# A PSUM bank for each half of the array's rows: dense products of a pre-LN block from paired turns to one list woven through attention scores

## The chip, the cores and the metric

The kernel runs on one core of a Trainium2 chip. The metric is the device time of one execution in microseconds, the median of the runs shown. The profiled execution is one further run of the same program, taken by the hardware profiler.

## What is computed

One transformer block in float32, for 2048 tokens of width 512: layer norm, attention with 32 query heads of width 16 that share one key and one value head, output projection and residual; then layer norm, a gated GELU feed-forward of width 1792 and residual.

```python
q = (x @ wq).reshape(B, S, H, Dh)           # x: layer norm of A_x; S 2048, D 512, H 32, Dh 16
k, v = x @ wk, x @ wv                       # one head for all 32
p = softmax(einsum("bhqd,bkd->bhqk", q, k) * Dh ** -0.5)
h = A_x + einsum("bhqk,bkd->bhqd", p, v).reshape(B, S, 512) @ wo
z = layernorm(h)
h2 = h + (gelu(z @ w_gate) * (z @ w_up)) @ w_down        # F 1792
```

## The kernel before

The 2048 query rows are handled in four **blocks** of 512. In a block, attention goes through 8 groups of 4 heads and, in a group, through 16 slices of 128 keys. A **score** (`scores`, two matmuls at L329, on rows 0 to 49 and 64 to 113 of the array at once, followed by one exponential of 128 x 1024 on ScalarE, L333) does two heads of one slice, so 32 scores make a group and 256 a block; the whole kernel has 1024. Scores go through two PSUM buffers of two banks each. `weigh` (L337) multiplies a finished pair of scores with the values, as 8 short matmuls into the one bank `acc`; at the end of a group `evacuate` copies `acc` (L350), sends it through DRAM to turn it (SP's DMAs at L351 and L361), and the sums are inverted, multiplied and split into a high and a low float32r part on VectorE (L366 to L383).

The **dense** part (`dense`) of a block is output projection, layer norm, transposes of the normalised rows (`x_turn`, L565), 14 slices of the feed-forward (`up`, a gate and an up product each), and the down products in runs of 4, 4, 4 and 2 slices. Products take each operand as high and low part, three terms for each chunk of 128 of the contraction. Weights are parted on GpSimd during block 0's attention, stored to DRAM (`w1_d`, `w2_d`) and loaded again for each block by SP (`load_w1`, `load_w2`, lines L470 and L475).

PE, ScalarE, GpSimd, and here SP and VectorE too, execute in the order in which the program issues. The dense part of block b is woven into the scores of block b + 1; that of the last block stands alone in the tail (`solo`, full array, L512; projection at L622). In the weave a matmul uses half of the array's 128 rows, and two run side by side. `duo` (L490) does two products at once: in the first turn rows 0 to 63 serve the first product's bank and rows 64 to 127 the second's, in the second turn it is the other way round, so that no bank is written by both halves at once. Between the turns VectorE reads one element of the second bank (`mark`, L498), which orders the turns; the turns lie in different **chunks**. A turn has 12 **steps** of two matmuls (6 for the last run of down products).

The order of the work around the change is written out in `run`: a group of 32 scores has six chunks of 6, 5, 5, 6, 5, 5 scores (`SIZES`), and `LONG`, `LAST` and `SHORT` say how many dense steps follow each score of a chunk. At the end of a chunk all finished pairs are weighed (`finish`), in the last chunk of a group all there are. The kinds of chunk of a block are a list: 4 long for the projection, one "gap" with transposes, the long ones of the feed-forward, 2 short. A block's dense part starts at chunk 3 of the next block for block 0 and at chunk 2 for the others (`LEAD`). `gates` (tanh on ScalarE, L690, and the products behind it, L691, L692, L112, L113) are opened at the end of the chunk after. Three PSUM banks (tag "d", `psum1`) serve the dense products; with four for scores and one for `acc` that makes eight.

The program runs on after the check of a bound (`bound_flag`); the second path, with exact maxima, isn't taken with these inputs.

Of the kernel before, what the change touches and what calls it, by code (L numbers as in the profile page):

```python
# [26 lines left out]
PB = 5  # L27
# [11 lines left out]
BOUND_STEPS = ((0, 10), (0, 14))  # L39

CUT, EDGE, GAP, HOLD = -1, -2, -3, -4
# [3 lines left out]
def kernel(  # L45
# [59 lines left out]
    w1_d = dram.tile([FC, P, 2, 2, DC, P], F32R, name="w1_d")  # L105
# [37 lines left out]
    def run(outer, first):  # L143
# [10 lines left out]
        def psum1(name):  # L154
            return ps.tile([P, T], F32, tag="d", bufs=width, name=name)
# [164 lines left out]
        o_blk, pair, outs, last_out = {}, [None], [], []  # L320
# [27 lines left out]
        def evacuate(b, g, acc):  # L348
            oT = sb.tile([P, T], F32, tag="oT", bufs=2, name=f"oT_{b}_{g}")
# [29 lines left out]
            def piece(t):  # L379
                sl = slice(t * P, (t + 1) * P)  # L380
                hi, lo = o_blk[b]
                invert(t)
                nc.vector.tensor_tensor(  # L383
                    oc[:, 0, sl], oc[:, 0, sl], oc[:, 1, sl], op=ALU.mult
                )
                split(nc.vector, hi[:, c, sl], lo[:, c, sl], oc[:, 0, sl])

# [4 lines left out]
            if b == NB - 1 and g == NG - 1:  # L392
                last_out.append(piece)
            elif k == 1:

                outs.extend([[] for _ in range(4 if b == 0 else 1)])
                outs.extend([partial(invert, t), partial(invert, t + 1)] for t in (0, 2))
                outs.append([divide])
            if b == 0 and g == NG - 1:
                while outs:  # L400
                    take_out()

# [3 lines left out]
        def part_weights(pw):  # L406
# [25 lines left out]
            def store_1(f, k, both):  # L432
                nc.gpsimd.dma_start(
                    w1_d[f, :, :, k].bitcast(F32),
# [33 lines left out]
        def load_w1(b, f):  # L468
            w = db.tile([P, 2, 2, DC, P], F32R, tag="w1", bufs=2, name=f"w1_{b}_{f}")
            nc.sync.dma_start(w.bitcast(F32), w1_d[f].bitcast(F32))  # L470
            return w[:, 0], w[:, 1]

        def load_w2(b, j):
# [4 lines left out]
            return w[:, :, 0], w[:, :, 1]  # L478

        def duo(names, terms):  # L480

            banks = [psum1(n) for n in names]
            n = len(terms[0])
            for turn in range(2):
                for i in range(n):
                    for a in range(2):
                        k = (turn + a) % 2
                        lhsT, rhs = terms[k][i]
                        rows = slice(64 * a, 64 * a + 64)
                        nc.tensor.matmul(  # L490
                            banks[k], lhsT[rows], rhs[rows], start=(turn == 0 and i == 0),
                            stop=(turn == 1 and i == n - 1), skip_group_check=True,
                        )
                    yield 1
                if turn == 0:

                    mark = sb.tile([P, 1], F32, tag="mark", bufs=2, name=f"mark_{names[1]}")
                    nc.vector.tensor_copy(mark, banks[1][:, :1])  # L498
                    yield CUT
            return banks  # L500

        tail_ps = None

        def tail_bank(name):
            return tail_ps.tile([P, T], F32, tag="t", bufs=5, name=name)

        def solo(names, terms):
            banks = []
            for name, ts in zip(names, terms):
                bank = tail_bank(name)  # L510
                for i, (lhsT, rhs) in enumerate(ts):
                    nc.tensor.matmul(bank, lhsT, rhs, start=(i == 0), stop=(i == len(ts) - 1))  # L512
# [4 lines left out]
        def dense(b, tail=False):  # L517

            o_hi, o_lo = o_blk[b]
            product = solo if tail else duo  # L520
            xbs = {}

            def load_x(t):
                xbs[t] = db.tile([P, D], F32, tag="xb", bufs=2, name=f"xb_{b}_{t}")
                nc.sync.dma_start(xbs[t], x_t[:, b * TB + t, :])

            if not tail:
                load_x(0)
                load_x(1)
            xT_hi = db.tile([P, DC, T], F32R, tag="x2h", bufs=1, name=f"x2h_{b}")  # L530
            xT_lo = db.tile([P, DC, T], F32R, tag="x2l", bufs=1, name=f"x2l_{b}")
            w1 = {0: load_w1(b, 0), 1: load_w1(b, 1)}
            if b == 0:
                yield 0
            w2 = {}
            hs, xns, held = {}, {}, {}

            def project(t0):
                terms = []
                for t in (t0, t0 + 1):  # L540
                    sl = slice(t * P, (t + 1) * P)
                    terms.append([
                        (ot[:, c, sl], wt[:, c, :])
                        for c in range(DC)
                        for ot, wt in ((o_hi, wo_hi), (o_hi, wo_lo), (o_lo, wo_hi))
                    ])
                banks = yield from product([f"pp_{b}_{t0}", f"pp_{b}_{t0 + 1}"], terms)
                held[t0], held[t0 + 1] = banks

            def residual(t0):  # L550
                for t in (t0, t0 + 1):
                    hs[t] = db.tile([P, D], F32, tag="h", bufs=4, name=f"h_{b}_{t}")
                    nc.vector.tensor_tensor(hs[t], held.pop(t), xbs.pop(t), op=ALU.add)
                scaled = []
                for t in (t0, t0 + 1):
                    xns[t] = db.tile([P, D], F32, tag="xn2", bufs=2, name=f"xn2_{b}_{t}")
                    scaled.append(layer_norm(db, xns[t], hs[t], f"2_{b}_{t}"))
                return scaled

            def x_turn(t):  # L560

                bank = tail_bank if tail else psum1
                pt = bank(f"pxt_{b}_{t}").rearrange("p (c q) -> p c q", c=DC)
# [4 lines left out]
                if tail:  # L568
                    first_part = partial(nc.scalar.activation, hi, pt, AF.Copy)
                else:  # L570
                    first_part = partial(nc.vector.tensor_copy, hi, pt)
                return first_part, partial(
# [3 lines left out]
            def start():  # L576
                yield from project(0)
                for step in residual(0):
                    step()
                load_x(2)  # L580
                load_x(3)
                yield CUT
                second = project(2)
                for n in second:
                    if n == CUT:
                        yield EDGE
                        for part in x_turn(0):
                            part()
                    yield n
                parts = x_turn(1)  # L590

                behind.extend([*residual(2), *parts])
                yield GAP
                two = [x_turn(t) for t in (2, 3)]
                for i in range(2):
                    for parts in two:
                        parts[i]()
                yield CUT

            def start_tail():  # L600

                xp, xn, h = (
                    sb.tile([P, TB, D], F32, tag="p", bufs=PB, name=f"{n}p_{b}")
                    for n in ("x", "xn", "h")
                )
                for t in range(TB):
                    nc.sync.dma_start(xp[:, t, :], x_t[:, b * TB + t, :])

                pps = [psum1(f"pp_{b}_0")]
                pps.extend(tail_bank(f"pp_{b}_{t}") for t in range(1, TB))  # L610

                def add_x(t):
                    nc.tensor.matmul(pps[t], ident, xp[:, t, :], start=False, stop=False)

                def project_part(t, cs, start):
                    terms = [
                        (ot[:, c, t * P : (t + 1) * P], wt[:, c, :])
                        for c in cs
                        for ot, wt in ((o_hi, wo_hi), (o_hi, wo_lo), (o_lo, wo_hi))
                    ]  # L620
                    for i, (lhsT, rhs) in enumerate(terms):
                        nc.tensor.matmul(  # L622
                            pps[t], lhsT, rhs, start=start and i == 0,
                            stop=not start and i == len(terms) - 1,
                        )

                def norm(t):
                    scaled[t] = layer_norm(db, xns[t], pps[t], f"2_{b}_{t}", on_act=True)

                piece, scaled = last_out.pop(), {}  # L630
                for t in range(TB):
                    hs[t], xns[t] = h[:, t, :], xn[:, t, :]
                    project_part(t, range(DC - 1), True)
                for t in range(TB):
                    piece(t)
                    add_x(t)
                    project_part(t, (DC - 1,), False)
                    if t == 2:
                        norm(0)
                for t in range(1, TB):  # L640
                    norm(t)
# [624 lines left out]
```

## Time and profile before

| | us |
|---|---|
| median of 3 runs | 1448.79 (1447.65 to 1449.84) |
| the profiled execution | 1448.96 |
| its span, first to last instruction | 1446.9 |
| PE busy in it | 1406.3 |
| ScalarE busy | 1038.8 |
| VectorE busy | 533.4 |

Mean granted TensorE clock in it: 0.999. Times in the profile are microseconds from the span's start unless marked ns. PE is TensorE's matmuls, PEld its weight loads, DVE VectorE, ACT ScalarE, POOL GpSimd, SP the engine that issues most DMAs. A group of instructions is a line with engine, operation, output<-inputs and count; then busy time and mean ns of one; then idle time of the engine just before them and what ended it. In a chain or a timeline the first two columns are start and duration. A matmul's duration (0.39 us) is longer than the distance to the next one, as they are pipelined.

### The profile page before, as it was taken

Reading aid. Unit: us, or ns where it says so; the run is one execution under the profiler, and the core shown is the slowest. Engines: PE = TensorE matmul, PEld = TensorE weight load, DVE = VectorE, ACT = ScalarE, POOL = GpSimd, SP = SyncE. Lnnn points to the kernel's source line nnn. Section 1 sums busy time; section 2 is a strip of 40 time slices with the busy share of each in tenths; the row PEclk is TensorE's granted clock in tenths of the full one; section 3 lists DMA queues with packets and bytes.
Section 4 is the critical chain, followed back from the end, with each engine's and each line's share of the span. In section 5 each row is a group of like instructions: output and inputs, shape, how many; then the busy total and the mean of one; then the engine's idle time right before and its main releaser. Section 6 shows DMA issues by size and latency. Waiting matters only on the chain.

```text
span 1446.9 us, 24766 instructions
## 1 busy us (share of the span) xinstructions
PE 1406.3 (97%) x10420; PEld 749.3 (52%) x10420; DVE 533.4 (37%) x925; ACT 1038.8 (72%) x1147; POOL 223.1 (15%) x305
## 2 busy tenths in 40 slices
PE   6999999999999999999999999999999999999998
PEld 5433333334555555554555555554555555556886
DVE  7403131223342424333242424323251422426665
ACT  6699999996777877777777777777777777772000
POOL 5588868601000000000000000000000000001000
PEclk9999999999999999999999999999999999999999
DMA  4467667631422333122333232212323323233552
GB/s 155 140 210 238 230 211 233 207 124 56 148 82 93 107 114 113 57 74 95 124 107 109 90 114 87 83 52 100 136 86 113 113 85 108 106 134 104 188 188 76
DMA packets 58863, 180.54 MB, mean 125 GB/s; under 512 B 8540, under 2 KB 8540, under 8 KB 51544
## 3 DMA queue, kind: packets, MB, share of 16 engines
q1 hardware_dynamic: 48912, 144.79, 29.6%
q0 software_dynamic: 9760, 34.08, 7.1%
q8 instruction: 84, 1.38, 0.4%
q14 instruction: 35, 0.29, 0.1%
q10 hardware_dynamic: 72, 0.00, 0.0%
HBM read 131.13 MB, written 47.71 MB: 124 GB/s over the span
## 4 chain that ended last, share of the span: by engine, by line
PE 76%; ACT 16%; issue 3%; DVE 2%; DMA 1%; POOL 0%; SPq 0%; ACTq 0%; POOLq 0%; DVEq 0%
PE acc L337 31%; PE s L329 17%; ACT p L333 15%; PE pu L490 5%; PE pd L490 5%; PE pg L490 4%; PE pq L182 3%; PE pd L512 3%; PE pg L512 2%; PE pu L512 2%; PE pp L490 1%; PE pk L1053 1%; DMA acc_d<-oT 1%; DVE oc L366 0%; DMA w<-w_d 0%
## 5 line engine op out<-in xcount | busy, mean ns | idle before, releaser
L333 ACT ACTIVATE p<-s 128x1024 f32<-128x1024 f32 x1024 | 967.8, 1036 | 257.6 <-PE s L329 257.1
L337 PE MATMUL acc<-p,v_sb 128*32 128x512 f32 x4096 | 493.9, 598 | 0.0
L329 PE MATMUL s<-qg,kaug 50*128 50x512 f32 x1984 | 391.5, 435 | 15.0 <-ACT p L333 11.1
L329 PEld LDWEIGHTS s<-qg,kaug 50*128 50x128 f32 x1984 | 169.8, 184 | 304.3 <-ACT p L333 173.2
L337 PEld LDWEIGHTS acc<-p,v_sb 128*32 128x32 f32 x4096 | 110.2, 109 | 240.4 <-issue 230.7
L490 PE MATMUL pu<-x2h,w 64*128 64x512 f32 x672 | 231.6, 391 | 0.0
L490 PE MATMUL pg<-x2h,w 64*128 64x512 f32 x672 | 231.5, 391 | 0.0
L122 POOL TENSOR_SCALAR rstd<-mv 128x1 f32<-128x1 f32 x16 | 3.5, 220 | 998.0 <-DVE mv L120 997.8
L490 PE MATMUL pg<-x2l,w 64*128 64x512 f32 x336 | 131.3, 391 | 0.0
L490 PE MATMUL pu<-x2l,w 64*128 64x512 f32 x336 | 131.3, 391 | 0.0
L490 PEld LDWEIGHTS pu<-x2h,w 64*128 64x128 f32 x672 | 124.9, 186 | 11.6
L490 PEld LDWEIGHTS pg<-x2h,w 64*128 64x128 f32 x672 | 124.8, 186 | 10.6
L490 PE MATMUL pd<-w,gh 64*128 64x512 f32 x672 | 105.4, 391 | 0.0
L690 ACT ACTIVATE ga<-ga 128x512 f32<-128x512 f32 x56 | 36.3, 647 | 89.6 <-DVE ga L685 89.6
L682 DVE COPY g<-pg 128x512 f32<-128x512 f32 x56 | 38.5, 688 | 128.5 <-PE pg L490 121.1
L490 PEld LDWEIGHTS pd<-w,gh 64*128 64x128 f32 x672 | 63.3, 185 | 14.6 <-issue 0.7
L366 DVE RECIPROCAL oc<-oc 128x128 f32<-128x128 f32 x64 | 56.0, 919 | 37.4 <-DMA oc<-acc_d 36.3
L498 DVE COPY mark_pu<-pu 128x1 f32<-128x1 f32 x42 | 6.6, 158 | 167.2 <-PE pu L490 167.2
L691 DVE SCALAR_TENSOR_TENSOR ga<-ga,g 128x512 f32<-128x512 f32 x56 | 38.8, 692 | 79.8 <-ACT ga L690 79.8
L490 PE MATMUL pd<-w,gl 64*128 64x512 f32 x336 | 66.4, 392 | 0.0
L490 PEld LDWEIGHTS pu<-x2l,w 64*128 64x128 f32 x336 | 62.4, 186 | 7.5
L490 PEld LDWEIGHTS pg<-x2l,w 64*128 64x128 f32 x336 | 62.4, 186 | 7.3
(235 smaller groups left out, 1279.5 us busy)
## 6 DMA issues: line engine op xcount, KB each, us to landing
w<-w_d SPq DMA_DIRECT2D x84, 1024.0 KB
qg<-q_d SPq DMA_DIRECT2D x62, 200.0 KB
q_d<-qh SPq DMA_DIRECT2D x32, 256.0 KB
acc_d<-oT SPq DMA_DIRECT2D x32, 256.0 KB
oc<-acc_d SPq DMA_DIRECT2D x128, 64.0 KB
w_d<-w_0b POOLq DMA_DIRECT2D x14, 512.0 KB, 3.1
w_d<-w_1b POOLq DMA_DIRECT2D x14, 512.0 KB, 4.4
x<-in_A_x_dram SPq DMA_DIRECT2D x16, 256.0 KB
```

Source lines behind the costliest of these rows:

```text
L182: nc.tensor.matmul(pq, wt[:, d, c * P : (c + 1) * P], xt[:, d, :], start=(n == 0), stop=(n == 3 * DC - 1),)
L329: nc.tensor.matmul(s[:, a, :], kaug[rows, kc * P : (kc + 1) * P], qg[rows, u, :], start=True, stop=True,)
L333: nc.scalar.activation(p[:, 2 * u : 2 * u + 2, :], s, AF.Exp, scale=SCALE)
L337: nc.tensor.matmul(acc[32 * j : 32 * j + 32, :], v_sb[:, kc, :], p[:, j, :], start=(kc == 0), stop=(kc == KC - 1), skip_group_check=True,)
L366: nc.vector.reciprocal(oc[:, 1, sl], oc[:, 1, sl])
L490: nc.tensor.matmul(banks[k], lhsT[rows], rhs[rows], start=(turn == 0 and i == 0), stop=(turn == 1 and i == n - 1), skip_group_check=True,)
L498: nc.vector.tensor_copy(mark, banks[1][:, :1])
L512: nc.tensor.matmul(bank, lhsT, rhs, start=(i == 0), stop=(i == len(ts) - 1))
L682: nc.vector.tensor_copy(g, pg)
L690: nc.scalar.activation(a, a, AF.Tanh, scale=GELU_A * GELU_C)
L691: nc.vector.scalar_tensor_tensor(a, a, 1.0, g, op0=ALU.add, op1=ALU.mult)
L1053: nc.tensor.matmul(pks[b], wt[:, c, :], xt[:, c, :], start=(c == 0 and n == 0), stop=(c == DC - 1 and n == 2),)
```

## The change

Each dense product now gets two banks, one for each half of the array's rows. `rows(0)` goes through a list of all products of three blocks (`queue_products`) on rows 0 to 63, `rows(1)` goes through the same list on rows 64 to 127, `LAG` = 6 steps behind. A step is one matmul of each. When a half is finished its bank is handed on (`spare`, a list of the three banks' tags, taken from the front) and VectorE reads it: the first half by a copy (for down products and projections an add to `h` or `x`), the second by an add. Marks, turns and the pairing of products are gone. Gate and up products are added up in SBUF tiles `g` and `u`; what follows them on VectorE (the cube for the GELU, the gate's operations, a norm) is put into a list `later`, from which two entries are taken after each finished half and at each cycle's start. Transposes (`turn`) take one of the same three banks.

The order is now a list of **cycles**: every 16 scores have three, with 5, 5 and 6 scores ("s") and 11, 11 and 14 steps ("d"); 3, 3 and 2 pairs are weighed ahead of them, whether or not a group ends there. Where fewer steps are available than a cycle holds (a block's first product waits for its part of the attention, and the first gate product for the four transposes) the cycle is a plain one of scores and weighings. The lead is 256 + 23 scores instead of 256 + 16. The projections of block b stand ahead of the last two down products of block b - 1.

Moved with it: w1 is stored and loaded in halves (gate, up) of 512 KB through three buffers, each load issued when the product three places ahead in the list ends; w2 is loaded when the last down product that reads its buffer ends; three residual inputs are loaded ahead instead of two; `oT` has one buffer instead of two; the division of a block's last two groups is done in quarters (`piece`) for every block but the first. Of block 2 the last two down products, 18 terms each, are done on the full array in the tail (`rest`), 18, 9 and 9 steps between the tail's transposes, where 6, 3 and 3 steps stood before.

```diff
-BOUND_STEPS = ((0, 10), (0, 14))
-CUT, EDGE, GAP, HOLD = -1, -2, -3, -4
+SUMS = ((0, 1, 2, 3), (4, 5, 6, 7), (8, 9, 10, 11, 12, 13))
+LAG = 6
+CYCLES = (
+    (3, "ssdddddsdddsddds", "vssvssvs"),
+    (3, "ssdddddsdddsddds", "vssvssvs"),
+    (2, "ssdddddsdddsdddsddds", "ssvssvss"),
+)
...
-    w1_d = dram.tile([FC, P, 2, 2, DC, P], F32R, name="w1_d")
+    w1_d = dram.tile([FC, 2, P, 2, DC, P], F32R, name="w1_d")
...
+        def take_bank(name):
+            tag = spare.pop(0)
+            return tag, ps.tile([P, T], F32, tag=tag, bufs=1, name=name)
...
-            oT = sb.tile([P, T], F32, tag="oT", bufs=2, name=f"oT_{b}_{g}")
+            oT = sb.tile([P, T], F32, tag="oT", bufs=1, name=f"oT_{b}_{g}")
...
-        def duo(names, terms):
-            banks = [psum1(n) for n in names]
-            n = len(terms[0])
-            for turn in range(2):
-                for i in range(n):
-                    for a in range(2):
-                        k = (turn + a) % 2
-                        lhsT, rhs = terms[k][i]
-                        rows = slice(64 * a, 64 * a + 64)
-                        nc.tensor.matmul(
-                            banks[k], lhsT[rows], rhs[rows], start=(turn == 0 and i == 0),
-                            stop=(turn == 1 and i == n - 1), skip_group_check=True,
-                        )
-                    yield 1
-                if turn == 0:
-                    mark = sb.tile([P, 1], F32, tag="mark", bufs=2, name=f"mark_{names[1]}")
-                    nc.vector.tensor_copy(mark, banks[1][:, :1])
-                    yield CUT
-            return banks
...
+        def up(b, f, k):
...
+            def done(a, bank):
+                tag = "gu"[k]
+                if a == 0:
+                    half = db.tile([P, T], F32, tag=tag, bufs=2, name=f"{tag}_{b}_{f}")
+                    nc.vector.tensor_copy(half, bank)
+                    halves[b, f, k] = half
+                else:
+                    half = halves[b, f, k]
+                    nc.vector.tensor_tensor(half, half, bank, op=ALU.add)
+                    load_w1(b * 2 * FC + 2 * f + k + 3)
+                    if k == 0:
+                        later.append(cube)
+                    else:
+                        later.append(lambda: tanhs.append((b, f)))
...
+        def rows(a):
+            nonlocal at
+            i = 0
+            while i < len(queue):
+                name, n, terms, done, ready = queue[i]
+                i += 1
+                if a == 0:
+                    assert ready is None or ready()
+                    left[0], at = n, i
+                    built.append([])
+                    source = iter(terms())
+                sent = built[i - 1]
+                tag, bank = take_bank(f"{name}_{a}")
+                r = slice(64 * a, 64 * a + 64)
+                for k in range(n):
+                    if a == 0:
+                        sent.append(next(source))
+                        left[0] -= 1
+                    lhsT, rhs, _ = sent[k]
+                    nc.tensor.matmul(
+                        bank, lhsT[r], rhs[r], start=(k == 0), stop=(k == n - 1),
+                        skip_group_check=True,
+                    )
+                    if k == n - 1:
+                        spare.append(tag)
+                        done(a, bank)
+                        side(2)
+                    yield
+
+        def step(first=True):
+            nonlocal ahead, clock
+            clock += 1
+            if first and next(firsts, 0) is None:
+                ahead += 1
+            if ahead > LAG or not first:
+                assert ahead > 0
+                next(seconds)
+                ahead -= 1
...
-        SIZES = (6, 5, 5, 6, 5, 5)
-        LEAD = (3, 2, 2)
-        n, lead = 0, 2 * PER + sum(SIZES[: LEAD[0]])
+        n, lead = 0, 2 * PER + 23
...
-        LONG = {5: (0, 5, 4, 3, 0), 6: (0, 5, 3, 3, 1, 0)}
-        LAST = (0, 5, 3, 1, 3)
-        SHORT = {5: (0, 6, 3, 3, 0), 6: (0, 6, 3, 3, 0, 0)}
...
+        for i in range(-((lead - end) // 16)):
+            if first and i in BOUND_LISTS:
+                bound_flag(BOUND_LISTS.index(i))
+            for count, woven, plain in CYCLES:
+                idle = available() < woven.count("d")
+                if idle:
+                    while available():
+                        step()
+                    if at == len(queue) or queue[at][0].startswith("pg"):
+                        catch_up()
+                bent = before(idle)
+                if not idle:
+                    finish(count)
+                for key in bent:
+                    later.extend(gate(*key))
+                for move in plain if idle else woven:
+                    if move == "d":
+                        step()
+                    elif move == "v":
+                        finish(1)
+                        clock += 4
+                    elif n < end:
+                        score(n)
+                        n += 1
+                        clock += 1
```

More of the change, by code (lines that the diff above doesn't have):

```diff
@@ L393, in evacuate @@
                 last_out.append(piece)
+            elif b > 0 and g == NG - 1:
+                outs.extend([partial(piece, t), partial(piece, t + 1)] for t in (0, 2))
             elif k == 1:
@@ L530, in dense, with last_dense @@
+        def last_dense():
+            b = NB - 1
+            o_hi, o_lo = o_blk[b]
+            xns, hb = {}, {}
             xT_hi = db.tile([P, DC, T], F32R, tag="x2h", bufs=1, name=f"x2h_{b}")
             xT_lo = db.tile([P, DC, T], F32R, tag="x2l", bufs=1, name=f"x2l_{b}")
[L532 to L558, printed above, removed]
@@ L567, in x_turn @@
                 hi, lo = xT_hi[:, :, sl], xT_lo[:, :, sl]
[L568 to L572, printed above, removed]
+                return partial(nc.scalar.activation, hi, pt, AF.Copy), partial(
                     nc.vector.tensor_tensor, lo, pt, hi.bitcast(F32), op=ALU.subtract
                 )
[L576 to L598, printed above, removed]
@@ L930, in run @@
         fixed.close()
-        assert not outs
+        assert not pend and not outs and at == len(queue) and left[0] == 0
         held_banks.close()
@@ L935, in run @@
         )
-        tail = dense(NB - 1, True)
+        tail, filling = last_dense(), rest()
         with tc.manual_schedule(engines={mybir.EngineType.DVE}):
+            catch_up()
+            side(100)
             assert next(tail) == HOLD
-            while next(work) != CUT:
-                pass
-            for _ in range(next(tail)):
-                assert next(work) == 1
-            assert next(tail) == HOLD
-            drain()
+            for steps in (18, 9):
+                for _ in range(steps):
+                    next(filling)
+                assert next(tail) == HOLD
+            for _ in filling:
+                pass
         for _ in tail:
```

500 lines of the change are left out of this document (310 added, 190 removed).

## The prediction, on record before the run

> **What bounds the kernel now.** First the page: shares of the span.
>
> ```profile
> span 1446.9 us, 24766 instructions
> PE 1406.3 (97%) x10420; PEld 749.3 (52%) x10420; DVE 533.4 (37%) x925; ACT 1038.8 (72%) x1147; POOL 223.1 (15%) x305
> PE 76%; ACT 16%; issue 3%; DVE 2%; DMA 1%; POOL 0%; SPq 0%; ACTq 0%; POOLq 0%; DVEq 0%
> ```
>
> PE is busy nearly throughout, but 16% of the chain that ended last is ScalarE: somewhere PE waits for exponentials. The sum is made against this execution: 1448.96 us, of which 1446.9 is the span; the median of the runs shown is 1448.79. A measurement of this kernel can tell about 0.2% (2.9 us) from no change.
>
> The change works between the first dense matmul and the tail. The timeline gives the ends of that stretch, and ScalarE's rate ahead of it:
>
> ```profile
> 311.63 9.28 ACT L333 ACTIVATE p<-s 128x1024 f32<-128x1024 f32 x10 [0.19 <-PE s L329]
> 319.46 0.40 PE L490 MATMUL pp<-wo_hi,o_hi 64*128 64x512 f32 x2
> 1301.47 0.50 PE L622 MATMUL pp<-wo_hi,o_hi 128*128 128x512 f32 x1
> ```
>
> The stretch lasts 982.0 us. One group of it (32 score pairs, 6 chunks) in the chain in order of time; each chunk starts with "acc":
>
> ```profile
> 744.04 2.71 PE acc L337 x24
> ...
> 750.97 2.71 PE acc L337 x24
> ...
> 758.26 2.71 PE acc L337 x24
> ...
> 765.36 0.50 PE s L329 x2
> 765.85 1.85 PE acc L337 x16
> 767.71 0.66 PE s L329 x4
> 768.37 1.16 PE pd L490 x10
> 769.52 0.29 PE s L329 x2
> ...
> 771.91 2.71 PE acc L337 x24
> ...
> 778.76 1.85 PE acc L337 x16
> ...
> 782.97 1.96 ACT p L333 x2
> 784.93 0.04 issue
> 784.98 0.50 PE s L329 x2
> 785.48 0.55 PE acc L337
> ```
>
> The group takes 785.48 - 744.04 = 41.44 us. Read its chunks as differences: 6.93, 7.29, 7.59, 6.06, 6.85, 6.72. A dense step (two half-array matmuls side by side) costs 1.16 / 5 = 0.232 us; I price a score pair the same. One more weighed pair (8 matmuls) costs 2.71 - 1.85 = 0.86. The smooth chunks (5 scores, 12 steps, three or two weighed pairs) take 6.89 (mean of 6.93 and 6.85) and 6.06, about 0.38 over their contents (17 x 0.232 + 0.86 each): entering and leaving the weighing. The other three hold the loss. Their last scores come one dense step after the one before, and ScalarE hasn't freed a score bank:
>
> ```profile
> 757.05 0.19 PEld L329 LDWEIGHTS s<-qg,kaug 50*128 50x128 f32 x2 [0.60 <-ACT p L333]
> 761.53 5.61 ACT L333 ACTIVATE p<-s 128x1024 f32<-128x1024 f32 x6 [2.19 <-PE s L329]
> 765.36 0.18 PEld L329 LDWEIGHTS s<-qg,kaug 50*128 50x128 f32 x2 [0.57 <-ACT p L333]
> ```
>
> ScalarE needs 5.61 / 6 = 0.935 us per score; 0.23 + 0.23 us of PE work lies between those two scores. Against smooth chunks of the same contents the three lose 7.29 - 6.89 = 0.40, 7.59 - 7.12 = 0.47 and 6.72 - 6.29 = 0.43: 1.30 us per group.
>
> **The change, part by part.**
>
> *The cadence.* From the order in which the built program's instructions stand: 135 woven cycles, every three holding 5, 5, 6 scores, 11, 11, 14 steps and 3, 3, 2 weighed pairs. Three dense steps and a score, 4 x 0.232 = 0.93, lie between later scores, against 0.935; no score follows one step after another, and none closes a group while its exponential is awaited. The long chunk of before, up to its fifth score, has this spacing and shows its wait only at the sixth. New cycles: 6.89 - 0.23 = 6.66 twice and 6.06 + 3 x 0.232 = 6.76, 20.08 per list, 40.16 per 32 scores: **1.28 us less per group**, 22.5 groups, 29 us.
>
> *The whole stretch.* Contents before by the order: 750 scores, 1644 steps, 378 weighed pairs, 147 weighings, 12 transpose sets (0.6 each, rough). 2394 x 0.232 + 378 x 0.86 + 147 x 0.38 + 7 = 943.6, so 38 us of 982.0 are waits: 29 the cadence, 9 at block boundaries. After: 743, 1620, 373, 148, 12: 932.4. To this come: first halves run alone for 6 steps at two starts and second halves at two ends, 24 matmuls x 0.116 = 2.8; 27 scores outside woven cycles, there still (the list crosses blocks, but waits for the last quarter of attention), at ScalarE's rate, 27 x 0.935 = 25.2 against about 22.7 of PE work: 2.5.
>
> *Banks.* Marks go; PE didn't wait for them (a mark is taken beside the weighing). In their place each product is read twice, by a copy and an add. Groups of instructions (count | busy, mean ns of one | idle before), and last the window of a busy group (PE, PEld, DVE, ACT, POOL busy):
>
> ```profile
> L490 PE MATMUL pu<-x2h,w 64*128 64x512 f32 x672 | 231.6, 391 | 0.0
> L498 DVE COPY mark_pu<-pu 128x1 f32<-128x1 f32 x42 | 6.6, 158 | 167.2 <-PE pu L490 167.2
> L682 DVE COPY g<-pg 128x512 f32<-128x512 f32 x56 | 38.5, 688 | 128.5 <-PE pg L490 121.1 <-PE pg L512 7.1
> L691 DVE SCALAR_TENSOR_TENSOR ga<-ga,g 128x512 f32<-128x512 f32 x56 | 38.8, 692 | 79.8 <-ACT ga L690 79.8
> L112 DVE CAST gh<-ga 128x512 fp32r<-128x512 f32 x56 | 23.9, 427 | 1.9
> 785.48:826.93 41.45, 41.02 (x340) 21.93 (x344) 17.46 (x28) 31.34 (x35) 0.00 (x0) 1.00 0.31 100
> ```
>
> VectorE in the mean has room: a busy group shows 17.5 of 41.45 us, and six products add 6 x 0.69 less six marks: 3.2 us. What counts is each place: with three banks, a bank is taken again 6 steps after its product ended, and if it's unread then PE stands, scores and weighing queued behind it, then ScalarE. One place by hand: in block 1, after the first half of gate 4, VectorE's list has copy, four gate operations, add: 0.69 + 0.69 + 0.69 + 0.43 + 0.69 + 0.69 = 3.9, with gaps 4.1; it begins 0.39 - 0.23 = 0.16 late and PE must hear of it (0.1 assumed): 4.4 us. PE has 12 steps and 3 scores ahead of the bank's next product: 15 x 0.232 = 3.5. It waits 0.9. The same sum along both orders at all 281 takings: in blocks 1 and 2 four waits of 0.9, one of 1.5, one of 2.0 (the first transposes, which take a bank of the same three behind a norm's stay on GpSimd), one of 0.7; 1.2 in block 0, where products fall differently against the weighings. **17 us**. Bounds: none (reads hide), and 67 if every read is 1.1 us later; 101 takings would then wait. I take 17, from the rows.
>
> The Trainium skill (TensorEngine Tiling (Array Packing), PSUM Bottleneck) speaks against the change: tiling speeds up the array but not the emptying of its banks, which may become the bottleneck. By that rule the gain would be eaten; the rows above say partly. That outcome is the second rival below.
>
> *Loads.* Gate and up weights come as 28 loads of 512 KB per block for 14 of 1 MB. Each is issued when its buffer's product ends, and due 18 steps later, about 10 us. A window of 4 us (last columns: DMA share, GB/s) and a row of the tail's chain:
>
> ```profile
> 372.00:376.00 4.00, 4.00 (x40) 2.43 (x40) 0.16 (x1) 4.00 (x5) 0.00 (x0) 1.00 1.02 418
> 1330.00 6.80 DMA w<-w_d
> ```
>
> At 418 GB/s, saturated, two 1 MB loads ahead of one take 6 us: hidden. Three stand ahead at a block's start, due 16 us later: hidden. Priming queues 5.2 MB instead of 2.5 ahead of the next queries on SP, 13 us, due about as late: nothing, at most 3. SP's waits are for readers just issued; GpSimd only stores differently shaped pieces. Uncovered, each late load would cost PE 1 to 3 us. The single output buffer refills once per group: nothing. The quarter divisions of a block's last heads lie beside score-only work; without that cover the projections would wait 1 to 2 us per block.
>
> *Lead and tail.* Seven scores more ahead of the stretch, at 9.28 / 10: +6.5. The tail receives 36 full-array steps instead of 12:
>
> ```profile
> 1316.53 0.73 PE L490 MATMUL pd<-w,gh 64*128 64x512 f32 x4
> 1321.45 0.66 PE L565 MATMUL pxt<-ident,xnp 128*128 128x128 f32 x4 [0.98 <-DVE x2l L651]
> 1323.34 0.73 PE L490 MATMUL pd<-w,gh 64*128 64x512 f32 x4
> 1324.23 2.11 PE L512 MATMUL pg<-x2h,w 128*128 128x512 f32 x8
> ```
>
> From 1316.53: 18 steps (4.2), transposes (1.1), 9 (2.1), transposes (1.2), 9 (2.1) end at 1327.2 instead of 1324.2, since part covers the waits for normalised rows: +3.0. The chain's 6.80 us load row made PE idle for part of its time; halves may save that or queue behind two 1 MB loads issued later than before. Bounds -1.5 and +2; I take -0.5, so +2.5.
>
> **Sum**: stretch 932.4 + 2.8 + 2.5 + 17 = 954.7, that is -27.3; +6.5, +2.5: -18.3. 1448.96 - 18.3 = **1430.7**.
>
> **The rivals.**
>
> 1. *Banks don't stall PE*: reads slip in, neighbouring waits merge. For it: VectorE under half busy; against: the hand sum. 1431 - 17 = 1414. Chance 0.22 for 1424 and below.
>
> 2. *VectorE's reads set the pace: slower.* Place: any second half whose add stands behind four gate operations or reciprocals. If every read comes 1.1 us later than in my sum, the waits are 67 instead of 17, +50: 1481. It decides from about 0.6 us of lateness, where the same sum gives 35 and the gain is used up. For it: 101 takings lie within 1.1 us, VectorE works strictly in order, and a reciprocal can stand waiting for its DMA. Against: the order gives that DMA a cycle more than before. Chance 0.17 for slower than 1452.
>
> 3. *ScalarE's waits come back*, as the new spacing is 0.93 against 0.935: if each 14-step cycle loses 0.43 at its sixth score, 45 x 0.43 = +19: 1450, no change. Against: the third score already waits for its bank (0.29 for 0.23 in its row), and the later ones are spaced from there. Chance 0.05 for within 0.2%; a part of it gives 1440 to 1446.
>
> That the change doesn't do what it says (boundaries still drain) is in the sum: three score-only phases remain.
>
> **How the numbers follow.** Forecast 1424 to 1446: chance 0.56. Faster by over 0.2%: 0.56 + 0.22 = 0.78; within: 0.05; slower: 0.17. The range 1412 to 1456 leaves out 0.15 to 0.2, nearly all above: it takes in zero bank waits below, and above rival 3 and the mild end of rival 2.
>
> **What would show it.** Group period about 40.2 plus bank waits; PE's waits for ScalarE gone from woven cycles; waits of PE for VectorE's copies and adds of pg, pu, pp, near 17 us in blocks 1 and 2, few in block 0; first pg of the tail 3 us later against the last weighing. Wrong if the period stays 41 or waits for VectorE stand in every cycle.

## The result, and the profile after

| | us | ratio to before, 95% interval |
|---|---|---|
| before, median of 12 runs | 1448.91 (1447.65 to 1450.30) | |
| changed, median of 12 runs | 1445.66 (1443.15 to 1446.86) | 0.9975 (0.9966 to 0.9984) |
| forecast | 1431 (range 1412 to 1456) | |

The change made the kernel faster by 0.25%, 3.3 us. The sign was as forecast and the time lies in the range, but only a fifth of the 18 us came. The profiled execution took 1446.27 us. Its page, the shares of the span:

```profile
span 1444.3 us, 25110 instructions
PE 1397.6 (97%) x10384; PEld 754.3 (52%) x10384; DVE 640.4 (44%) x1043; ACT 1031.0 (71%) x1147; POOL 218.7 (15%) x305
PE 86%; DVE 6%; ACT 3%; DMA 2%; issue 1%; POOL 1%; SPq 0%; ACTq 0%; DVEq 0%; POOLq 0%
```

ScalarE's part of the chain that ended last fell from 16% to 3%: what the change was to remove is gone. VectorE's rose from 2% to 6%. The timeline of PE in the changed kernel gives the ends of the parts (start, duration):

```profile
327.54 0.40 PE L742 MATMUL pp<-wo_hi,o_hi 64*128 64x512 f32 x1
...
1291.82 0.50 PE L825 MATMUL pp<-wo_hi,o_hi 128*128 128x512 f32 x1
...
1317.12 0.62 PE L772 MATMUL pg<-x2h,w 128*128 128x512 f32 x2
```

| part | before | changed | difference | forecast |
|---|---|---|---|---|
| start to first dense matmul | 319.46 | 327.54 | +8.1 | +6.5 |
| the stretch, to the first projection on the full array | 982.0 | 964.3 | -17.7 | -27.3 |
| from there to the first gate product | 22.8 | 25.3 | +2.5 | +3.0 |
| from there to the end of the span | 122.7 | 127.2 | +4.5 | -0.5 |

So the forecast lost 9.6 us in the stretch, 1.6 ahead of it and 4.5 behind it. The stretch first. A list of 16 scores (three cycles) in the chain of the changed kernel, in block 0's steady part:

```profile
556.53 2.71 PE acc L358 x24
...
563.24 1.85 PE acc L358 x16
...
569.99 2.71 PE acc L358 x24
...
576.63 2.71 PE acc L358 x24
```

576.63 - 556.53 = 20.10 us, against 20.08 forecast; the cadence is not what failed. Measured from the first exponential of each list to that of the next, all lists of the stretch (us):

```
changed   24.72 20.00 20.10 20.25 20.07 20.06 20.11 20.09 20.05 20.04 20.07 20.10 20.06 20.05 19.17 22.72
          25.76 20.06 20.73 21.15 20.71 20.08 20.05 20.31 20.71 20.08 20.07 20.14 20.80 20.08 18.31 22.77
          25.78 20.07 20.73 21.13 20.72 20.10 20.07 20.11 20.70 20.08 20.09 20.08 20.72 20.08
```

Two kinds of list are longer than 20.08. Where a block ends, three lists take 67.65 and 66.86 us together, and the stretch's first takes 24.72. In the steady parts of blocks 1 and 2 some lists take 0.65 or 1.05 more, 7.7 us in sum. PE's waits in this execution (us in total, times, longest) name the engines:

```profile
PE pxt L575 <- DVE xb L554: 10.7, 8, 2.1
PE s L350 <- ACT p L354: 3.5, 10, 0.7
PE pxt L575 <- DVE h L562: 3.1, 2, 1.6
PE pg L742 <- DVE g L616: 3.1, 8, 0.4
PE pu L772 <- DMA w<-w_d: 2.3, 3, 1.1
PE pd L742 <- DVE h L672: 1.4, 3, 0.5
PE pg L742 <- DVE u L612: 1.2, 2, 0.6
```

The two rows of "pxt", the transposes, hold 13.8 us. Block 1's first transposes in the timeline of the changed kernel, VectorE, GpSimd and PE (in brackets the idle time before, and what ended it):

```profile
647.49 0.69 DVE L565 TENSOR_TENSOR h<-h,pp 128x512 f32<-128x512 f32 x1 [0.95 <-PE pp L742]
648.21 0.69 DVE L130 BATCH_NORM_STATS2 st<-h 128x6 f32<-128x512 f32 x1
648.94 0.18 DVE L131 BATCH_NORM_AGGREGATE mv<-st 128x2 f32<-128x6 f32 x1
650.13 0.55 DVE L554 TENSOR_SCALAR xb<-h,mv,rstd 128x512 f32<-128x512 f32 x1 [1.01 <-POOL rstd L134]
650.59 0.68 DVE L562 TENSOR_TENSOR h<-pp,xb 128x512 f32<-128x512 f32 x1
...
649.52 0.57 POOL L134 TENSOR_TENSOR rstd<-rstd,power 128x1 f32<-128x1 f32 x1
...
651.33 0.66 PE L575 MATMUL pxt<-ident,xb 128*128 128x128 f32 x4 [1.56 <-DVE h L562]
```

The second half of the projection ends ahead of 647.49. From there to the normalised row at 650.68 are 3.2 us on VectorE and GpSimd, and VectorE, in order, stands 1.01 of them with the next product's add (L562) queued behind. The transposes come at the next cycle's start, PE has nothing else to do in its order, and stands 1.56 us.

Two waits end here, one behind the other. The row is there at 650.68; but by the program's order this first set takes the bank that L562 still reads, until 651.27, and it is this read that the row names. The first set of block 2 does the same (1.54 us). In the other eight waits, 10.7 us, the normalised row itself (`xb`) comes last, as at the first set of block 0:

```profile
339.83 0.66 PE L575 MATMUL pxt<-ident,xb 128*128 128x128 f32 x4 [2.13 <-DVE xb L554]
```

Ten of the twelve sets wait. In the kernel before only two did, for 1.2 us in all; the row of its waits in the stretch:

```profile
PE pxt L565 <- DVE xn L927: 1.2, 2, 0.6
```

### The profile page after: what moved, and what is told of

The parts are those of the page before. It is cut to its first block, busy times and chain, and to the rows that moved or that the text cites. A ratio compares the mean times of both kernels' runs of the same rounds, so it can differ in the third digit from the quotient of the medians.

```text
span 1444.3 us, 25110 instructions
## 1 busy us (share of the span) xinstructions
PE 1397.6 (97%) x10384; PEld 754.3 (52%) x10384; DVE 640.4 (44%) x1043; ACT 1031.0 (71%) x1147; POOL 218.7 (15%) x305
## 4 chain that ended last, share of the span: by engine, by line
PE 86%; DVE 6%; ACT 3%; DMA 2%; issue 1%; POOL 1%; SPq 0%; ACTq 0%; DVEq 0%; POOLq 0%
PE acc L358 31%; PE s L350 19%; PE pg L742 8%; PE pd L742 7%; PE pu L742 6%; PE pq L203 3%; PE pd L772 3%; ACT p L354 3%; PE pu L772 2%; PE pg L772 2%; PE pp L742 2%; DMA w<-w_d 1%; PE pd_rest L784 1%; DVE st L130 1%; PE pxt L575 0%
## 5 line engine op out<-in xcount | busy, mean ns | idle before, releaser
L354 ACT ACTIVATE p<-s 128x1024 f32<-128x1024 f32 x1024 | 960.5, 1040 | 254.5 <-PE s L350 254.2
L742 PE MATMUL pg<-x2h,w 64*128 64x512 f32 x672 | 177.4, 394 | 4.2 <-DVE g L616 3.1
L742 PE MATMUL pu<-x2h,w 64*128 64x512 f32 x672 | 175.3, 394 | 0.0
L672 DVE TENSOR_TENSOR h<-h,pd 128x512 f32<-128x512 f32 x80 | 54.3, 685 | 151.7 <-PE pd L742 151.7
L742 PEld LDWEIGHTS pg<-x2h,w 64*128 64x128 f32 x672 | 96.1, 186 | 20.5 <-DVE g L616 6.6
L742 PE MATMUL pg<-x2l,w 64*128 64x512 f32 x336 | 100.7, 392 | 0.0
L742 PEld LDWEIGHTS pu<-x2h,w 64*128 64x128 f32 x672 | 94.3, 186 | 11.2
L742 PE MATMUL pu<-x2l,w 64*128 64x512 f32 x336 | 99.2, 392 | 0.0
L879 ACT ACTIVATE ga<-ga 128x512 f32<-128x512 f32 x14 | 8.9, 632 | 94.5 <-DVE ga L876 94.5
L616 DVE TENSOR_TENSOR g<-g,pg 128x512 f32<-128x512 f32 x42 | 28.8, 685 | 91.1 <-PE pg L742 91.1
L616 DVE TENSOR_TENSOR u<-u,pu 128x512 f32<-128x512 f32 x42 | 28.9, 688 | 78.9 <-PE pu L742 78.7
```

The source lines that it names most:

```text
L354: nc.scalar.activation(p[:, 2 * u : 2 * u + 2, :], s, AF.Exp, scale=SCALE)
L616: nc.vector.tensor_tensor(half, half, bank, op=ALU.add)
L672: nc.vector.tensor_tensor(hs[b, t], hs[b, t], bank, op=ALU.add)
L742: nc.tensor.matmul(bank, lhsT[r], rhs[r], start=(k == 0), stop=(k == n - 1), skip_group_check=True,)
```

## The experiments

**The changed kernel again.**

> The changed kernel once more, nothing edited, for one more profile. Two numbers of its first profile are in doubt: the tail's full-array step (233 ns, against 226.5 in the kernel before) and the start of the dense work (8.1 us later, where 7 more scores make 6.5). If the step belongs to the program, it is 233 again and the tail from its first gate product to the end is 127 us again; if it belongs to the execution, it may be 226.5 and the tail 124. If the lead's extra 1.6 us was a moment of that execution, the first dense matmul stands at about 326 instead of 327.5.

1444.94 us, span 1442.9. The tail's step is 233 ns again: it belongs to the program. The dense work begins at 326.25, +6.8 against the first profile of before, near the 6.5 of the forecast. But the second list begins where it did (352.5 against 352.2): the 1.6 us only came later. A window of the first profile, and one of the second (behind the PE, PEld, DVE, ACT and POOL columns stands the granted clock):

```profile
308.00:312.00 4.00, 3.88 (x18) 0.78 (x19) 0.00 (x0) 2.82 (x4) 0.00 (x0) 0.59 0.17 62
```
```profile
338.00:344.00 6.00, 5.50 (x32) 2.59 (x34) 2.72 (x5) 0.90 (x1) 0.00 (x0) 0.72 0.17 46
```

In the first the clock fell in the lead, in the second behind the wait of 2.1 us for the first transposes. The first profile has the same wait, 2.13 us at 339.83, and there the clock stayed at 1.00:

```profile
338.00:344.00 6.00, 4.17 (x35) 2.21 (x36) 3.11 (x5) 2.11 (x4) 0.81 (x2) 1.00 0.18 48
```

**Transposes one cycle later.** The transposes may follow the normalising 12 counts later instead of 6, which at each block's end is the next cycle:

```diff
-                if clock - scaled_at[b_t] < LAG:
+                if clock - scaled_at[b_t] < (LAG if idle else 12):
```

> Each set of transposes is issued one cycle (6.7 us) later. Theory (the missing gain stands at the block boundaries: TensorE stands 13.8 us in front of transposes whose normalised rows VectorE and GpSimd have not finished): most of this goes, the boundary lists of 22.7 and 25.8 us fall towards 21 and 21.5, the time by about 12 us, to 1434. What stays is the first of them in block 0, up to 2 us. Rival 1 (it is the three banks that are short, as the prediction had it): the wait moves to the next product that takes a bank, and the time stays within 3 us of 1445.7. Rival 2 (the first gate product of the next block now comes before its rows): score-only cycles appear, and the time stays or grows by some us.

1430.84 us, ratio 0.9881 (0.9866 to 0.9897): 14.8 us less than the changed kernel by the medians, 13.6 by the ratios, a little more than the theory's 12. PE's waits now:

```profile
PE s L350 <- ACT p L354: 3.7, 11, 0.7
PE pg L742 <- DVE g L616: 3.1, 8, 0.4
PE pd L742 <- DVE h L672: 1.4, 3, 0.5
```

Both "pxt" rows are gone, the product rows are what they were (3.1, 1.4, and 1.2 for u). The block ends take 19.14 + 20.53 + 21.84 = 61.5 us instead of 67.65. Rival 1 falls: a bank shortage would have shown in the product rows. The two waits for a bank at the first sets went too, as a cycle later it has been read. Rival 2 falls too: the gate products wait for nothing more.

**The add ahead of the split.** The steady lists' waits, in the timeline of VectorE and PE of the changed kernel:

```profile
713.96 0.69 DVE L612 COPY g<-pg 128x512 f32<-128x512 f32 x1 [0.17 <-PE pg L742]
714.57 0.68 DVE L634 SCALAR_TENSOR_TENSOR ga<-ga,g 128x512 f32<-128x512 f32 x1
715.28 0.69 DVE L635 TENSOR_TENSOR ga<-ga,u 128x512 f32<-128x512 f32 x1
716.00 0.43 DVE L123 CAST gh<-ga 128x512 fp32r<-128x512 f32 x1
716.47 0.69 DVE L124 TENSOR_TENSOR gl<-ga,gh 128x512 fp32r<-128x512 f32 x1
717.08 0.68 DVE L616 TENSOR_TENSOR g<-g,pg 128x512 f32<-128x512 f32 x1
...
717.81 0.49 PE L742 MATMUL pg<-x2h,w 64*128 64x512 f32 x1 [0.38 <-DVE g L616]
```

This is the place that the prediction worked by hand: copy, four gate operations, add. Only two of the four go ahead of the add in this version; TensorE's order is the same.

```diff
                         done(a, bank)
-                        side(2)
+                        side(1 if later and later[0].__name__ == "weigh_up" else 2)
```

> VectorE takes two instead of four gate operations between the first half's copy and the second half's add, so the add comes 1.1 us sooner; TensorE's order is unchanged. Theory (the steady lists' waits of 0.65 and 1.05 us, about 8 us in sum, are banks that stand unread behind the four gate operations): most of them go, 1440. Rival (those waits have another releaser, or the time only moves to the next read): within 2 us of 1445.7.

1439.38 us, ratio 0.9935 (0.9921 to 0.9948): 6.3 less by the medians, 5.8 by the ratios. The lists of 20.7 become 20.07 to 20.16; two of 21.01 stay, where two reciprocals (1.76 us) stand in VectorE's list. Over 20.08 the steady lists are 2.2 us in sum instead of 7.7. The theory holds.

**Both.** The two edits together.

> Both edits that made the changed kernel faster, together: transposes one cycle later (14.8 us by itself) and the second half's add ahead of the split (6.3 us by itself). If the two losses are separate, as the theory says (one at the block boundaries, one in the steady lists), they add up: 1445.7 - 14.8 - 6.3 = 1424.6. Rival (both take the same wait on VectorE's list): 1429 to 1431, as with the later transposes alone.

1425.27 us, ratio 0.9828 (0.9814 to 0.9841). The losses are separate and add up.

**The old spacing.** The cycles get the kernel before's spacing:

```diff
-    (3, "ssdddddsdddsddds", "vssvssvs"),
-    (3, "ssdddddsdddsddds", "vssvssvs"),
-    (2, "ssdddddsdddsdddsddds", "ssvssvss"),
+    (3, "ssdddddsddddsddds", "vssvssvs"),
+    (3, "ssdddddsddddsddds", "vssvssvs"),
+    (2, "ssdddddsdddsdddsds", "ssvssvss"),
```

> The two-bank list stays, but the cycles get 12 steps each and the spacing of the kernel before (5, 4, 3 steps between scores, and 5, 3, 3, 1 in the cycle of six). Theory (the cadence is what the change earns, 0.65 us per list of 16 scores): the list goes from 20.07 to about 20.7, 45 of them make +29 us, 1475, slower than the kernel before, since lead, tail and boundaries stay as they are. Rival (the list that is not drained earns by itself, and ScalarE gets ahead at its own rate whatever the spacing): the list stays near 20.1 to 20.3 and the time under 1456.

1452.15 us, ratio 1.0018 (1.0008 to 1.0027): slower than before, but by far less than the theory's 1475, and in the rival's range. The lists fit neither's number; the chain of this run, one list:

```profile
750.13 2.71 PE acc L358 x24
...
757.06 1.85 PE acc L358 x16
...
760.30 1.65 ACT p L354 x2
...
762.11 1.06 ACT p L354
...
763.72 2.71 PE acc L358 x24
...
770.59 2.71 PE acc L358 x24
```

770.59 - 750.13 = 20.46, not 20.72. One cycle of the three, the one with a single step between its last two scores, waits for ScalarE. The expectation had miscounted: the kernel before has three such close pairs per 32 scores, this version two. And the bank waits of the steady lists went: all but one (20.72) take 20.44 to 20.48, none 0.65 more. Products have 12 steps, and so have these cycles; each half ends at about the same place in its cycle, which may be why, but was not tested by itself. By lists: 38 steady ones are 14.7 us over 20.08 in sum instead of 7.7, 7 more; the two ratios differ by 0.43%, 6.2 us.

**The old spacing with all three close pairs.** Every other list gets a cycle "ssdddddsdddsdsddd" in its middle.

> The two-bank list with all three of the close pairs of scores that the kernel before has per 32 scores, where the run called old_spacing had only two: every other list has a cycle of five scores with 5, 3, 1 and 3 steps between them. Theory (each close pair loses about 0.4 us, and nothing else in the cadence counts): lists of 20.47 and about 20.87 in turn, 41.34 per 32 scores where the kernel before has 41.44; 22 such pairs make +9, about 1461. Rival (part of the kernel before's loss was the draining of the list at each pair of products): 20.47 everywhere, 1452.

1461.31 us, ratio 1.0075 (1.0061 to 1.0089): +0.57% against the version with two, 8 us, as the theory has it; the lists take about 20.46 and 20.88 in turn. So a close pair costs 0.4 us, and the spacing alone carries the cadence's gain; that the list isn't drained earns little in the steady parts (41.34 us per 32 scores here, 41.44 in the kernel before).

**Late reads.** One more VectorE operation ahead of every read of a bank:

```diff
                         spare.append(tag)
+                        again = db.tile([P, 6], F32, tag="again", bufs=1, name=f"again_{name}_{a}")
+                        nc.vector.bn_stats(again, bank)
                         done(a, bank)
```

> The changed kernel, with one more VectorE operation of about 0.69 us ahead of each read of a bank (statistics of the bank, which nothing uses), 288 times: every read is that much later. The prediction's sum gave 17 us of bank waits as it stands and about 35 when every read is 0.6 us late. Theory (few takings are near their limit now, many within 1 us): the bank waits grow by 18 to 25, the transposes' by about 0.7 to 1.4 each, 10 of them: 1470 to 1480. Rival (a later read is mostly hidden, and only the chain ahead of the transposes feels it): 1452 to 1458.

1488.32 us, ratio 1.0244 (1.0219 to 1.0269): 39 us more than the changed kernel by the ratios. The profile has 272 added operations, not the expectation's 288. In the profiled execution (1490.86 us, 44.6 more than the changed kernel's) the steady lists are 28.8 us over 20.08 in sum instead of 7.7: +21, inside the theory's 18 to 25. The lists at the block ends took 24.5 us more, where 7 to 14 were expected. The waits for transposes grew within that, by 7.9 to 21.7. The timeline of PE of this run, and windows of it, show what came on top:

```profile
340.60 1.12 PE L575 MATMUL pxt<-ident,xb 128*128 128x128 f32 x4 [2.73 <-DVE xb L554]
341.64 3.64 PE L358 MATMUL acc<-p,v_sb 128*32 128x512 f32 x16
```
```profile
340.00:346.00 6.00, 5.40 (x24) 2.00 (x26) 2.57 (x4) 0.00 (x0) 0.00 (x0) 0.50 0.17 46
...
353.00:358.00 5.00, 5.00 (x31) 1.39 (x31) 2.05 (x4) 0.00 (x0) 0.00 (x0) 0.66 0.19 63
```

After 2.73 us of idle PE the granted clock is 0.50 for six us; 16 weighing matmuls take 3.64 us instead of 1.85. The same is seen at 660 to 700, at 860 to 880 and at 1000 to 1040 us of this run (0.83 to 0.91 over each 20 us). In the whole stretch the trace has the clock at half for 37.5 us, at most 18.8 us of lost time, nearly all at the block ends; the changed kernel's first profile has none there. A wait can be paid twice.

**The tail's step.** The tail's products of 12 terms, PE's timeline before, and changed:

```profile
1339.78 1.98 PE L512 MATMUL pu<-x2h,w 128*128 128x512 f32 x8
...
1342.50 1.98 PE L512 MATMUL pg<-x2h,w 128*128 128x512 f32 x8
```
```profile
1334.74 2.03 PE L772 MATMUL pg<-x2h,w 128*128 128x512 f32 x8
...
1337.54 2.03 PE L772 MATMUL pu<-x2h,w 128*128 128x512 f32 x8
```

2.72 / 12 = 226.7 ns a step, and 2.80 / 12 = 233.3, for the same matmuls on the same terms. The kernel before once more:

> The kernel before, nothing edited, for a second profile of the tail. If the full-array step of 226.5 ns belongs to its program, it is 226 to 227 again; if it belonged to that execution, it may be 233, as in the changed kernel.

1448.94 us; the step is 226.5 ns again. It goes with the program. What differs between the programs is where the operands lie in SBUF. First, in the version with both edits, 64 bytes more in the attention pool:

```diff
         def prime():
+            nc.vector.memset(sb.tile([P, 16], F32, tag="pad", bufs=1, name="pad"), 0.0)
```

> The combined version with 64 bytes more in the pool that held the marks of the kernel before, so that the projections' stationary operands stand at the same places in SBUF as there; the gate, up and down products' operands stay where they were. It asks why a full-array step of the tail takes 233 ns in all versions with the new list and 226.5 ns in both profiles of the kernel before. If the place of the stationary operand decides, the projections' step is 226.5 and that of the products after them still 233. If it doesn't, both stay at 233, the time stays at 1425, and the cause stays open.

1422.71 us (one run): projections 227 ns, the products behind them still 233, side by side in one execution. The addresses of the compiled programs, as the difference of stationary and moving operand, modulo 256 bytes, with the step of the tail:

| | o and wo: projections | w1 and x2: gate, up | gate parts and w2: down |
|---|---|---|---|
| before | 0: 227 ns | 0: 227 | 0: 227 |
| changed, and the versions above but late reads | 64: 233 | 128: 233 | 128: 233 |
| late reads (its added tile moves the dense pool) | 64: 233 | 96: 234 | 160: 233 |
| 64 bytes more | 0: 227 | 128: 233 | 128: 233 |

The 64 bytes were the marks' tiles, which the change removed; the 128 come from its new order of tiles in the dense pool. In the changed kernel alone, both put right:

```diff
+            nc.vector.memset(sb.tile([P, 16], F32, tag="pad", bufs=1, name="pad"), 0.0)
             for i in range(3):
...
             for j in range(3):
                 load_w2(0, j)
+            nc.vector.memset(db.tile([P, 32], F32, tag="gap", bufs=1, name="gap"), 0.0)
```

> The changed kernel with 64 bytes more in the attention pool and 128 bytes more in the dense pool, between the weight tiles and the normalised rows; nothing else is edited. In the programs compiled so far a full-array step took 226.5 ns wherever the two operands' addresses in SBUF differ by a multiple of 256 bytes, and 233 ns where they differ by 64 or 128 more. The two gaps make it a multiple of 256 for the projections and for the gate, up and down products. If the place decides: 226.5 ns in the whole tail, some 550 steps there, 3.6 us less, 1442; if the half-array steps gain too, up to 2 us more, 1440. If it doesn't decide: 233 ns for gate, up and down, 1445.5.

1440.50 us, ratio 0.9946 (0.9932 to 0.9959), against 0.9975: 4 to 5 us less. The timeline of this run's tail:

```profile
1327.25 1.98 PE L774 MATMUL pg<-x2h,w 128*128 128x512 f32 x8
...
1329.97 1.98 PE L774 MATMUL pu<-x2h,w 128*128 128x512 f32 x8
```

2.72 again. The half-array steps gain too: over some 2290 distances of consecutive pairs in each trace the mean goes from 233.56 to 232.25 ns, which over the 1620 steps is 2.1 us. And the other way round, in the kernel before, with 128 bytes between normalised rows and gate and up weights:

```diff
+            if b == 0:
+                nc.vector.memset(db.tile([P, 32], F32, tag="gap", bufs=1, name="gap"), 0.0)
             w1 = {0: load_w1(b, 0), 1: load_w1(b, 1)}
```

> The kernel before with a gap of 128 bytes between the normalised rows and the gate and up weights, so that their addresses differ by 128 more than a multiple of 256; projections and down products keep their differences of 0. If the place decides: in the tail 233 ns for gate and up products and still 226.5 ns for projections and down products, the time up by about 336 x 6.6 ns = 2.2 us. If not: 226.5 ns throughout.

1450.19 us (one run). The timeline of its tail:

```profile
1342.21 2.02 PE L512 MATMUL pg<-x2h,w 128*128 128x512 f32 x8
...
1345.01 2.02 PE L512 MATMUL pu<-x2h,w 128*128 128x512 f32 x8
...
1356.10 0.62 PE L512 MATMUL pd<-w,gh 128*128 128x512 f32 x2
...
1358.82 0.62 PE L512 MATMUL pd<-w,gh 128*128 128x512 f32 x2
```

Gate to up is 2.80 for 12 steps; the down products, whose difference stayed 0, take 1358.82 - 1356.10 = 2.72 for 12. The half-array steps go from 232.1 to 233.0 ns in the mean. The place decides.

**All three.** Later transposes, the add ahead of the split, operands placed.

> Later transposes, the add ahead of the split, and the operands placed: 1425.3 less 3.6 for the tail's steps gives 1421.7; 1420 if the half-array steps gain as well; 1425 if the place of gate, up and down operands is not what matters.

1418.63 us, ratio 0.9795 (0.9781 to 0.9808): 2.0% faster than the kernel before, eight times the gain of the change as it was made.

## Why the prediction was right in sign and wrong in size

- **Cadence: right.** 20.08 us per list forecast, 20.04 to 20.11 measured, and for the reason given: a close pair of scores costs 0.4 us, shown by putting two and three of them back. Rival 3 (ScalarE's waits return) didn't come.
- **Bank waits of products: mechanism right, too large.** The 17 us held 13 for products. Measured 7.7, most of it behind the four gate operations, as the hand-worked place had it; moving the add left 2.2. The curve behind rival 2 held: reads 0.7 us later cost the steady lists 21 us more, and with the block ends the kernel was 2.4% slower than before. The Trainium skill's rule (TensorEngine Tiling (Array Packing), PSUM Bottleneck) agrees in part with this trace: in the steady lists banks that aren't yet read take 7.7 us of the cadence's gain of 29, not all.
- **Transposes: the step that failed.** "The same sum along both orders at all 281 takings" followed the banks, and gave the first transposes of blocks 1 and 2 a bank wait of 2.0 each, 4 in all. These two came, 1.56 and 1.54 us. What the sum put at nothing, without a reason, is the wait for the operand, the normalised rows: add, statistics, GpSimd's root, scaling, 3.2 us from the product's end, due at the next cycle's start for each of the four sets of a block. That made eight waits more, 10.7 us; together ten waits, 13.8 us, and removing them brought 14 to 15.
- **Step time: a term that was missing.** The prediction took 0.232 us from before for the stretch and nothing for the tail's products. The change moved the operands: 2.1 us in the stretch by the half-array steps, 3.3 in the tail by some 500 steps x 6.6 ns. That was the greater part of the tail's +4.5, where -0.5 was taken for loads. Waits for w1 in the tail are 2.3 us against 1.5 before (1.0 and none in the second profiles): part of the loads' bounds, and no gain.
- **Lead and rest: right.** +6.8 in the second profile for +6.5; +2.5 for +3.0 between the first projection and the first gate product.

That 1445.7 lies in the forecast's 1424 to 1446 all the same is luck: it lies at the edge, and neither the transposes' operands nor the tail's step is in the sum or its range.

The stretch's 9.6 us: transposes 13.8 - 4 = +9.8, products 7.7 - 13 = -5.3, half-array steps +2.1; 3.0 are not assigned.

## What to carry to other kernels

When a drained schedule becomes one list, waits that the old order covered can be exposed (for transposes 1.2 us before, 13.8 after): follow each moved instruction's operands to their last producer across all engines, not only the buffer that it takes. A wait of PE that sits at a fixed point of a hand-written order is often removed by issuing the waiting instruction one cycle later, where something else is ready. After any edit that adds or removes tiles, compare the time of an untouched matmul: here a removed 64-byte tile and a new tile order cost 4 to 5 us, more than the change earned.

## What the runs showed of the hardware

- A full-array float32r step of 512 columns takes 226.7 ns where the addresses of its two operands differ by a multiple of 256 bytes, and 233 to 234 ns where they differ by 64, 96, 128 or 160 more. Seen in every version measured, in both directions, and for two kinds of product in one execution. The rule by 256 bytes is read from these differences alone; others weren't tried, and why is open.
- The granted clock can fall after short idle times of PE: to 0.50 after 2.73 us (late reads), and in the changed kernel's second profile behind a wait of 2.1 us (0.72 over 6 us). The Trainium skill (TensorE: Matmul & The Clock Gate, Part 1: The HAM clock gate) gives about 3.4 us for an idle window that halves the clock; the half agrees with 0.50, the time here was shorter. Waits of 1.5 us at the block ends of the changed kernel left the clock at 1.00, and so did the wait of 2.13 us in its first profile. In late reads the clock halved beside each of the five waits of 2.2 us and more, and beside some of those from 1.5 to 1.8 us. So these runs give no length of wait that decides.
